# Joining the small matmul bursts of a fused attention and Winograd-MoE kernel: values and next scores side by side at eleven of fifteen places

## The chip, the cores and the metric

The kernel runs on one core of a Trainium2 chip. The metric is the device time of one execution in microseconds (us). The kernel before took 674.62 us (median of three runs, 672.25 to 675.16). A smaller number is better.

## The reference

Eight batches of eight heads of attention over 576 positions, head size 64, with one of two sparse causal masks: heads 0 to 3 look back at most 31 positions (local), heads 4 to 7 look at positions with the same remainder by 32 (strided). The result goes through a layer with three input matrices, an elementwise maximum and one output matrix.

```python
def _attn_ref(q, k, v):
    B, H, S, D = q.shape                      # 8, 8, 576, 64
    stride, scale = 32, 1.0 / np.sqrt(D)
    scores = scale * np.matmul(q, k.transpose(0, 1, 3, 2))
    ...
    mask_local = (rel >= 0) & (rel < stride)
    mask_strided = (rel >= 0) & (pos[None, :] % stride == pos[:, None] % stride)
    ...
    scores = np.where(masks[None, :, :, :], scores, -1000000000.0)
    scores = scores - np.max(scores, axis=-1, keepdims=True)
    attn = np.exp(scores)
    attn = attn / (np.sum(attn, axis=-1, keepdims=True) + 1e-09)
    return np.matmul(attn, v).astype(np.float32)

def _moe_ref(x, w1, w2, w3, w_out):           # x: 4608 x 512, d_ff 768
    h = np.maximum(np.maximum(x @ w1, x @ w2), x @ w3)
    return (h @ w_out).astype(np.float32)
```

## The kernel before

**Units.** The attention is cut into 32 units, unit n being batch n // 4 and one pair of heads; units with n % 4 of 0 and 1 are strided, with 2 and 3 local. A unit goes through these steps, each a function of the kernel:

- `scores(n)`: a burst of 64 small matmuls (strided, line 314, tiles of 64 rows x 64 columns of the array) or 72 (local, line 336, 64 x 32) into the one PSUM tile `s_ps`;
- `less_maximum(n)` on DVE: add the mask (L357), take the maximum (L365), subtract it (L366);
- `exponentials(n)` on ACT (L382);
- `probabilities(n)` and `transposed(n)` on DVE: sum (L393), two small steps (L394, L395), multiply (L396), transpose into `pt` (L403), after which `s_ps` is free for the next unit;
- `values(n)`: a burst of 64 small matmuls (strided, L469, tiles 64 x 64) or 84 (local, L440, 32 x 64) into `o_ps`;
- `leading(n)` on ACT: copies of `o_ps` to the block of the layer's input (L494).

Ahead of a strided unit's scores, `paired_queries` makes four copies on ACT (L291).

**Supers.** Tokens 1024 to 4607 go through the layer in four supers of 896 tokens. A super has nine quads, and a quad is seven products (a Winograd form of a 2 x 2 block product), so a super has 63 products, numbered k = 0 to 62. One product is six matmuls of 128 x 128 weights against 448 columns (line 788). Products alternate between two PSUM banks, and ACT copies each result out (`snap`, L835, or L842): a product two places on writes the same bank and waits for that copy. The fourth, fifth and sixth products of a quad (k % 7 of 3, 4, 5) also have an addition on POOL (L847) behind the copy; in quads with q % 3 of 1 or 2 DVE takes a running maximum (L849) after that addition, and after the copy of the seventh. After quad 7 (after product 55) `split` casts two pieces of the hidden layer on ACT (L872) and DVE (L873). After the 63 products come the 126 output matmuls of a super (L882), with the conversion of the next super's input beside them.

**Order.** Every instruction is pinned to the order in which the program is written, on each engine. What places the late units (16 to 31) among the products is `before(s, k)`, called ahead of product k of super s, and `after(s, k)`, called behind it and ahead of that product's copy. With `COUNTS = (6, 6, 4, 0)`, `before` puts the scores of unit n + 1 ahead of product 8, 17, 26, 35, 44 and 53 (`k % 9 == 8`, lines 799 to 803) and the values of unit n one product later (lines 804 and 805). `after` puts the exponentials two products behind the scores, the probabilities and the transpose three behind, and the paired queries four behind (lines 811 to 817). Loads of queries, keys and values go out on SP's queue beside these steps, between the loads of the products' weights (`load_next`), which run eight ahead.

Of the kernel before, what the change touches and what calls it, by code (L numbers as in the profile page):

```python
# [37 lines left out]
NBLOCK = (B * S - PLAIN) // BL  # L38
NSUPER = NBLOCK // 2
AHEAD = 8  # L40
COUNTS = (6, 6, 4, 0)
W_LEAST = 2.0**-15
W_MOST = 122877.984375
NKC = DM // P
# [26 lines left out]
def fused_kernel(ctx, tc, qT, kT, qk_loc, qk_str, v_loc, v_str, m_loc, m_str, w1, w2, w3, w_out, out):  # L71
# [158 lines left out]
    units = [(b, p) for b in range(B) for p in (2, 3, 0, 1)]  # L230
# [420 lines left out]
    def ahead(n):  # L651

        scores(n)
        list(load_qk(n + 2))
        less_maximum(n)
# [66 lines left out]
    coming, since = None, 0  # L722
# [59 lines left out]
    def supers():  # L782
# [9 lines left out]

        def before(s, k):

            n = 16 + sum(COUNTS[:s]) + (k - 8) // 9
            if s == 0 and k == 1:
                ahead(16)
                running[:] = [16, k]
            elif k % 9 == 8 and k // 9 < COUNTS[s]:
                running[:] = []  # L800
                if n + 1 < len(units):
                    ahead(n + 1)
                    running[:] = [n + 1, k]
            elif k and k % 9 == 0 and k // 9 <= COUNTS[s]:
                placed(n)

        def after(s, k):

            if running:
                n, since = running  # L810
                if k == since + 2:
                    exponentials(n)
                if k == since + 3:
                    probabilities(n)
                    transposed(n)
                if k == since + 4 and n + 1 < len(units) and (n + 1) % 4 in (0, 1):
                    paired_queries(n + 1)

        def quad(s, q):
            _, j, i = builds[q]  # L820
# [69 lines left out]
            pin(nc.scalar.dma_start(out=out[r : r + P, :], in_=o_sb))  # L890

        running = []
        for s in range(NSUPER):
            for q in range(9):
                quad(s, q)
                if q == 7:
                    split(0, 0, 4)
                    split(1, 0, 4)
            split(2, 0, 4)
            split(0, 4, 6)  # L900
            split(1, 4, 6)
            split(2, 4, 6)
            convert = conversion(s + 1) if s + 1 < NSUPER else iter(())
            out_part(0, 0, 4)
            out_part(1, 0, 4)
            for t in range(7):
                out_part(t, 0 if t > 1 else 4, 6)
                store(s, t)
                if t < 4:
                    split(t + 3, 0, 6)  # L910
                next(convert, None)
            list(convert)
# [68 lines left out]
```

## Time and profile before

| | |
|---|---|
| median of three runs | 674.62 us (672.25 to 675.16) |
| the profiled execution | 670.4 us, of which the span of instructions is 668.6 us |
| PE (matmul) busy | 644.8 us, 96% of the span |
| PE weight loads busy | 552.2 us, 83% |
| DVE, ACT, POOL busy | 372.6, 336.6, 300.0 us: 56%, 50%, 45% |
| line 788, the products | 1512 matmuls, 317.4 us |
| granted TensorE clock, mean | 0.989 |

The profiled execution is 4.2 us below the median of the three runs. The page's busy time of PE counts matmuls from their start to a modelled end, and these overlap, so the distances from start to start in a timeline say more than busy shares. PE, DVE, ACT, POOL and SP are the engines; PEld is PE's weight load, which runs beside matmuls. A super's products stand at 203 to 296 us, 325 to 417, 446 to 531 and 560 to 636 of the span; the late units stand in the first three.

### The profile page before, as it was taken

How to read it: one execution, taken by the hardware profiler on the slowest of the kernel's cores; microseconds unless marked ns; L12 is line 12 of the kernel's file. 1: busy time of each engine (PE TensorE's matmuls, PEld its weight loads, DVE VectorE, ACT ScalarE, POOL GpSimd, SP SyncE). 2: the span in 40 equal slices, each digit the busy share in tenths (PEclk: the TensorE clock that was granted, in tenths of full speed). 3: DMA queues.
4: the chain of work that ended last, by engine and by line, in shares of the span. 5: the costliest groups of instructions: out<-in, count | busy, mean ns of one | idle time of the engine just before them, and what ended most of it. 6: DMA issues, size and time to landing. Idle time of an engine off the chain costs nothing.

```text
span 668.6 us, 18029 instructions
## 1 busy us (share of the span) xinstructions
PE 644.8 (96%) x7408; PEld 552.2 (83%) x7408; DVE 372.6 (56%) x515; ACT 336.6 (50%) x702; POOL 300.0 (45%) x291
## 2 busy tenths in 40 slices
PE   4589999999999999999999999999999999999997
PEld 3467888878778888888888888888899888999986
DVE  5887877576675566476255756643652562214240
ACT  5767566335264455456445455544454554444441
POOL 7879999699942334230224233004324401444410
PEclk9789999999999999999999999999999999999999
DMA  9989885657699778761477898228767614777411
GB/s 291 271 231 367 269 257 177 210 165 234 188 296 334 248 245 276 238 228 63 132 240 256 227 296 250 75 96 223 229 175 212 204 63 125 216 217 216 125 47 64
DMA packets 89370, 138.36 MB, mean 207 GB/s; under 512 B 10152, under 2 KB 39592, under 8 KB 89288
## 3 DMA queue, kind: packets, MB, share of 16 engines
q1 hardware_dynamic: 85256, 129.86, 63.0%
q10 hardware_dynamic: 4032, 7.34, 2.9%
q8 instruction: 59, 0.97, 0.6%
q14 instruction: 23, 0.19, 0.1%
HBM read 111.21 MB, written 25.95 MB: 205 GB/s over the span
## 4 chain that ended last, share of the span: by engine, by line
PE 93%; ACT 2%; DVE 1%; issue 1%; DMA 1%; POOL 1%; SPq 1%; DVEq 0%; ACTq 0%; POOLq 0%
PE f_ps L788 46%; PE f_ps L882 17%; PE f_ps L521 15%; PE f_ps L551 4%; PE o_ps L440 3%; PE o_ps L469 2%; PE s_ps L314 2%; PE s_ps L336 2%; DMA w<-in_w 1%; ACT s_ps L374 1%; DVE o_ps L179 0%; DVE work L182 0%; DMA v_t<-in_v_loc 0%; PE o_ps L480 0%; SPq L265 0%
## 5 line engine op out<-in xcount | busy, mean ns | idle before, releaser
L788 PE MATMUL f_ps<-xc,w_stream 128*128 128x448 f32 x1512 | 317.4, 368 | 0.2 <-ACT snap L835 0.2
L788 PEld LDWEIGHTS f_ps<-xc,w_stream 128*128 128x128 f32 x1512 | 280.5, 188 | 26.3 <-ACT snap L835 1.8
L835 ACT COPY snap<-f_ps 128x448 f32<-128x448 f32 x240 | 128.0, 534 | 164.6 <-PE f_ps L788 162.4
L847 POOL TENSOR_TENSOR snap<-snap 128x448 f32<-128x448 f32 x72 | 88.9, 1240 | 148.8 <-ACT snap L835 122.5
L849 DVE TENSOR_TENSOR h_all<-h_all,snap 128x448 f32<-128x448 f32 x96 | 81.1, 886 | 128.9 <-POOL snap L847 128.9
L847 POOL TENSOR_TENSOR h_all<-snap 128x448 f32<-128x448 f32 x36 | 41.4, 1150 | 167.5 <-ACT snap L835 166.3
L882 PE MATMUL f_ps<-wNone,h_parts 128*128 128x512 f32 x504 | 115.0, 389 | 0.0
L882 PEld LDWEIGHTS f_ps<-wNone,h_parts 128*128 128x128 f32 x504 | 94.6, 188 | 19.6
L521 PE MATMUL f_ps<-xh,w 128*128 128x512 f32 x288 | 95.1, 401 | 0.4 <-issue 0.4
L521 PEld LDWEIGHTS f_ps<-xh,w 128*128 128x128 f32 x288 | 54.7, 190 | 13.0 <-issue 0.6
L521 PE MATMUL f_ps<-xl,w 128*128 128x512 f32 x144 | 56.8, 394 | 0.4 <-DVE xl L499 0.4
L873 DVE TENSOR_TENSOR h_parts<-h_all,h_parts 128x768 fp32r<-128x768 f32 (+2 forms) x40 | 27.2, 712 | 30.3 <-ACT h_parts L872 30.2
L888 ACT COPY work<-f_ps 128x512 f32<-128x512 f32 x28 | 16.4, 587 | 46.1 <-PE f_ps L882 46.1
L685 DVE TENSOR_TENSOR xc<-x_block,xc 128x896 fp32r<-128x896 f32 x28 | 29.8, 1087 | 11.7 <-ACT xc L682 11.7
L393 DVE TENSOR_REDUCE s_ps<-s_ps 128x10 f32<-128x640 f32 (+2 forms) x30 | 23.1, 772 | 19.4 <-ACT s_ps L382 19.4
L403 DVE STREAM_TRANSPOSE pt<-s_ps 128x640 f32<-128x640 f32 (+2 forms) x32 | 32.5, 1016 | 1.2
L521 PEld LDWEIGHTS f_ps<-xl,w 128*128 128x128 f32 x144 | 27.3, 190 | 5.9 <-DVE xl L499 0.7
L382 ACT ACTIVATE s_ps<-s_ps 128x640 f32<-128x640 f32 (+2 forms) x30 | 19.5, 649 | 22.2 <-DVE s_ps L366 22.2
L872 ACT CAST h_parts<-h_all 128x768 fp32r<-128x768 f32 (+2 forms) x40 | 24.5, 643 | 12.1 <-DVE h_all L849 5.5
L551 PE MATMUL f_ps<-wNone,hh 128*128 128x512 f32 x96 | 30.6, 400 | 0.0
L682 ACT CAST xc<-x_block 128x896 fp32r<-128x896 f32 x28 | 25.7, 943 | 5.4 <-DVE x_block L688 3.0
L336 PEld LDWEIGHTS s_ps<-qk_t 64*32 64x32 f32 x1408 | 16.2, 114 | 14.2 <-issue 13.5
(87 smaller groups left out, 680.2 us busy)
## 6 DMA issues: line engine op xcount, KB each, us to landing
w_stream<-scratch SPq DMA_DIRECT2D x252, 256.0 KB, 3.5
w<-in_w SPq DMA_DIRECT2D x18, 512.0 KB, 7.5
qk_t<-in_qT SPq DMA_DIRECT2D x28, 288.0 KB, 3.5
qk_t<-in_kT SPq DMA_DIRECT2D x28, 288.0 KB, 5.3
v_t<-in_v_str SPq DMA_DIRECT2D x56, 128.0 KB, 4.5
out<-work ACTq DMA_DIRECT2D x28, 256.0 KB, 2.0
scratch<-w SPq DMA_DIRECT2D x27, 256.0 KB, 3.8
v_t<-in_v_loc SPq DMA_DIRECT2D x48, 96.0 KB, 3.9
```

What stands on the lines that cost most here:

```text
L336: pin(nc.tensor.matmul(s_ps[32 * j : 32 * (j + 1), h, k1 : k1 + w], t[hs, q0 : q0 + 32], t[hs, k0 : k0 + w], start=not first, stop=not fir ...
L403: pin(nc.vector.transpose(pt[:, :, : nm * at], s_ps[:, :, : nm * at]))
L521: pin(nc.tensor.matmul(f_ps, w[:, kc, :], x[:, kc, :], start=(kc == 2 and n == 0), stop=(kc == 1 and n == 2)))
L551: pin(nc.tensor.matmul(f_ps, h[:, ts], w, start=(j == 0 and n == 0), stop=(j == NJ - 1 and n == 2)))
L682: pin(nc.scalar.copy(out=x[m][:, 0], in_=src))
L685: pin(nc.vector.tensor_tensor(out=x[m][:, 1], in0=src, in1=x[m][:, 0].bitcast(F32), op=ALU.subtract))
L788: pin(nc.tensor.matmul(out_, w[:, wl, fs], x[:, xl, k, :], start=start and k == 0 and n == 0, stop=k == 1 and n == 2, skip_group_check=not ...
L835: pin(nc.scalar.copy(out=t, in_=src))
L847: pin(nc.gpsimd.tensor_tensor(out=h if i == 0 else u, in0=u, in1=t, op=ALU.add))
L849: pin(nc.vector.tensor_tensor(out=h, in0=h, in1=u, op=ALU.max))
L873: pin(nc.vector.tensor_tensor(out=to[:, 1, j0:j1], in0=src, in1=to[:, 0, j0:j1].bitcast(F32), op=ALU.subtract))
L882: pin(nc.tensor.matmul(outs[t], h, w, start=(j == 0 and n == 0), stop=(j == NJ - 1 and n == 2)))
```

## The change

`COUNTS` goes; two tables of numbers, `SCORES_AT` and `VALUES_AT`, say per super ahead of which product a unit's scores and a unit's values stand, the units numbered from 16 in the order of the tables. Where the same product stands in both tables (11, 24, 44, 54 in super 0; 11, 27, 47, 57 in super 1; 10, 18, 29 in super 2), `before` now issues the values of unit n and then the scores of unit n + 1 with nothing between them; behind both come the loads of values, the copies of `leading`, the loads of queries and keys, and `less_maximum`. At the four other places (units 18 and 19, 21 and 22, 23 and 24, 25 and 26) the scores still come first and one product stands between. Within a super the scores of a unit stand 7 to 13 products behind those of the unit before. The scores of unit 22 and values of unit 21 move from the end of super 0 to the start of super 1. The arithmetic is unchanged. Line numbers after the change are up to nine higher (788 is 789, 314 is 315, 469 is 470).

```diff
--- before.py
+++ after.py
@@ -38,7 +38,8 @@
 NBLOCK = (B * S - PLAIN) // BL
 NSUPER = NBLOCK // 2
 AHEAD = 8
-COUNTS = (6, 6, 4, 0)
+SCORES_AT = ((1, 11, 24, 33, 44, 54), (0, 11, 18, 27, 36, 47, 57), (10, 18, 29))
+VALUES_AT = ((11, 24, 34, 44, 54), (1, 11, 19, 27, 37, 47, 57), (10, 18, 29, 37))
 W_LEAST = 2.0**-15
 W_MOST = 122877.984375
 NKC = DM // P
@@ -792,17 +793,19 @@
 
         def before(s, k):
 
-            n = 16 + sum(COUNTS[:s]) + (k - 8) // 9
-            if s == 0 and k == 1:
-                ahead(16)
-                running[:] = [16, k]
-            elif k % 9 == 8 and k // 9 < COUNTS[s]:
-                running[:] = []
-                if n + 1 < len(units):
-                    ahead(n + 1)
-                    running[:] = [n + 1, k]
-            elif k and k % 9 == 0 and k // 9 <= COUNTS[s]:
-                placed(n)
+            n, new = values_at.get((s, k)), scores_at.get((s, k))
+            if n is not None:
+                values(n)
+            if new is not None:
+                scores(new)
+                running[:] = [new, k]
+            if n is not None:
+                list(load_v(n + 2))
+                leading(n)
+                rest(n)
+            if new is not None:
+                list(load_qk(new + 2))
+                less_maximum(new)
 
         def after(s, k):
 
@@ -815,6 +818,8 @@
                     transposed(n)
                 if k == since + 4 and n + 1 < len(units) and (n + 1) % 4 in (0, 1):
                     paired_queries(n + 1)
+                if k == since + 4:
+                    running.clear()
 
         def quad(s, q):
             _, j, i = builds[q]
@@ -890,6 +895,10 @@
             pin(nc.scalar.dma_start(out=out[r : r + P, :], in_=o_sb))
 
         running = []
+        scores_at, values_at = (
+            {at: 16 + i for i, at in enumerate((s, k) for s, ks in enumerate(places_) for k in ks)}
+            for places_ in (SCORES_AT, VALUES_AT)
+        )
         for s in range(NSUPER):
             for q in range(9):
                 quad(s, q)
```

Three places where the order of instructions moves:

On PE in super 0, the first place with two bursts before (ahead of products 8 and 9): L788 is a product, L314 the scores of unit 17, L469 the values of unit 16.

```order
L788 MATMUL f_ps_781<-xc_2966,w_stream 128x448 x6
L314 MATMUL s_ps<-qk_t,pt 64x2x18 x32
L788 MATMUL f_ps_782<-xc_2967,w_stream 128x448 x6
L469 MATMUL o_ps<-pt,v_t 64x2x18 x32
L788 MATMUL f_ps_781<-xc_2968,w_stream 128x448 x6
L788 MATMUL f_ps_782<-xc_2969,w_stream 128x448 x6
L788 MATMUL f_ps_781<-xc_2970,w_stream 128x448 x6
```

The same two bursts after the change, ahead of product 11 (product 8 is the first row):

```order
L789 MATMUL f_ps_782<-xc_2967,w_stream 128x448 x6
L789 MATMUL f_ps_781<-xc_2968,w_stream 128x448 x6
L789 MATMUL f_ps_782<-xc_2969,w_stream 128x448 x6
L470 MATMUL o_ps<-pt,v_t 64x2x18 x32
L315 MATMUL s_ps<-qk_t,pt 64x2x18 x32
L789 MATMUL f_ps_781<-xc_2970,w_stream 128x448 x6
L789 MATMUL f_ps_782<-xc_2971,w_stream 128x448 x6
```

The product that stood between the bursts now stands outside, the values come first, and both bursts are of tiles 64 x 64.

On ACT around product 55 of super 0, before: L494 the copies of unit 21, L382 the exponentials of unit 22, L872 the two casts behind quad 7, L835 the copies of products.

```order
L494 COPY x_block_3347<-o_ps 128x384
L494 COPY x_block_4130<-o_ps 128x192
L835 COPY snap<-f_ps_782 128x448
L382 ACTIVATE s_ps<-s_ps 128x2x320
L835 COPY snap<-f_ps_781 128x448
L872 CAST h_parts<-h_all 128x512 x2
L835 COPY snap<-f_ps_782 128x448
```

After the change, where unit 21 has its scores ahead of product 54 (L495 the copies of unit 20, L383 the exponentials of unit 21, L877 the casts):

```order
L495 COPY x_block_3330<-o_ps 128x384
L495 COPY x_block_4187<-o_ps 128x192
L840 COPY snap<-f_ps_782 128x448
L840 COPY snap<-f_ps_781 128x448
L877 CAST h_parts<-h_all 128x512 x2
L383 ACTIVATE s_ps<-s_ps 128x32x18
L840 COPY snap<-f_ps_782 128x448
L840 COPY snap<-f_ps_781 128x448
```

The casts and the exponentials had a copy of a product between them; now they stand back to back, with the copy of product 56 behind both.

On DVE in super 1, unit 23 before (L357 to L366 its maximum, L849 the running maximum of the hidden layer, L393 to L403 its probabilities and transpose), with its scores ahead of product 8:

```order
L357 TENSOR_TENSOR s_ps<-s_ps,mloc 128x2x320
L365 TENSOR_REDUCE mx<-s_ps 128x2x5
L366 TENSOR_TENSOR s_ps<-s_ps,mx 128x2x320
L849 TENSOR_TENSOR h_all<-h_all,snap 128x448
L393 TENSOR_REDUCE s_ps<-s_ps 128x2x5
L394 TENSOR_SCALAR s_ps<-s_ps 128x2x5
L395 RECIPROCAL sm<-s_ps 128x2x5
L396 TENSOR_TENSOR s_ps<-s_ps,sm 128x2x320
L403 STREAM_TRANSPOSE pt<-s_ps 128x2x320
L849 TENSOR_TENSOR h_all<-h_all,snap 128x448 x3
```

After the change, with its scores ahead of product 11:

```order
L854 TENSOR_TENSOR h_all<-h_all,snap 128x448
L358 TENSOR_TENSOR s_ps<-s_ps,mloc 128x2x320
L366 TENSOR_REDUCE mx<-s_ps 128x2x5
L367 TENSOR_TENSOR s_ps<-s_ps,mx 128x2x320
L854 TENSOR_TENSOR h_all<-h_all,snap 128x448 x3
L394 TENSOR_REDUCE s_ps<-s_ps 128x2x5
L395 TENSOR_SCALAR s_ps<-s_ps 128x2x5
L396 RECIPROCAL sm<-s_ps 128x2x5
L397 TENSOR_TENSOR s_ps<-s_ps,sm 128x2x320
L404 STREAM_TRANSPOSE pt<-s_ps 128x2x320
L854 TENSOR_TENSOR h_all<-h_all,snap 128x448
```

One running maximum (of product 10) now stands ahead of the unit's own maximum, and three (of products 11, 12, 13) instead of one ahead of its probabilities.

## Rows read from the trace of the kernel before

**Rows 1.** The page: busy time of each engine (share of the span, instructions), and the share of the chain of waits that ended last, by engine.

```profile
PE 644.8 (96%) x7408; PEld 552.2 (83%) x7408; DVE 372.6 (56%) x515; ACT 336.6 (50%) x702; POOL 300.0 (45%) x291
...
PE 93%; ACT 2%; DVE 1%; issue 1%; DMA 1%; POOL 1%; SPq 1%; DVEq 0%; ACTq 0%; POOLq 0%
```

**Rows 2.** The waits of PE's matmuls, and then of its weight loads, from 204 to 640 us: engine, line, waited for; us in total, times, the longest.

```profile
PE f_ps L788 <- ACT snap L835: 0.2, 1, 0.2
```

```profile
PEld o_ps L469 <- issue: 2.5, 8, 0.3
...
PEld f_ps L788 <- ACT snap L835: 1.8, 6, 0.5
```

**Rows 3.** The timeline of PE around two places in super 0 (start, length with the modelled end, instructions merged): the scores of units 21 and 22, the values of units 20 and 21.

```profile
268.39 1.14 PE L314 MATMUL s_ps<-qk_t,pt 64*64 64x36 f32 x64
269.46 1.50 PE L788 MATMUL f_ps<-xc,w_stream 128*128 128x448 f32 x6
270.89 1.14 PE L469 MATMUL o_ps<-pt,v_t 64*64 64x36 f32 x64
271.95 9.99 PE L788 MATMUL f_ps<-xc,w_stream 128*128 128x448 f32 x48
281.88 0.97 PE L336 MATMUL s_ps<-qk_t 64*32 64x64 f32 x72
282.78 1.49 PE L788 MATMUL f_ps<-xc,w_stream 128*128 128x448 f32 x6
284.19 1.14 PE L469 MATMUL o_ps<-pt,v_t 64*64 64x36 f32 x64
```

**Rows 4.** The same view of super 3, whose 63 products have no burst among them.

```profile
559.64 76.78 PE L788 MATMUL f_ps<-xc,w_stream 128*128 128x448 f32 x378
636.26 1.09 PE L882 MATMUL f_ps<-wNone,h_parts 128*128 128x512 f32 x4
```

**Rows 5.** The same view at 58 us, in an earlier stage of the kernel, where two small bursts of the same tile stand side by side (L521 is that stage's large matmul).

```profile
58.25 1.14 PE L314 MATMUL s_ps<-qk_t,pt 64*64 64x36 f32 x64
59.20 1.12 PE L469 MATMUL o_ps<-pt,v_t 64*64 64x36 f32 x64
60.25 0.50 PE L521 MATMUL f_ps<-xh,w 128*128 128x512 f32 x1
```

**Rows 6.** The timeline of ACT from product 54 of super 1 (idle time and its releaser in brackets): exponentials of unit 28, casts behind quad 7, paired queries.

```profile
407.37 0.53 ACT L835 COPY snap<-f_ps 128x448 f32<-128x448 f32 x1 [0.52 <-PE f_ps L788]
407.80 0.65 ACT L382 ACTIVATE s_ps<-s_ps 128x576 f32<-128x576 f32 x1
408.64 0.53 ACT L835 COPY snap<-f_ps 128x448 f32<-128x448 f32 x1 [0.20 <-PE f_ps L788]
409.07 1.15 ACT L872 CAST h_parts<-h_all 128x512 fp32r<-128x512 f32 x2
410.12 0.53 ACT L835 COPY snap<-f_ps 128x448 f32<-128x448 f32 x1
410.54 1.34 ACT L291 COPY pt<-qk_t 128x288 f32<-128x288 f32 x4
411.77 1.01 ACT L835 COPY snap<-f_ps 128x448 f32<-128x448 f32 x2
```

**Rows 7.** The waits of the weight loads in the stretch of rows 6 (402 to 414 us) and in the one around unit 23 (334 to 350 us).

```profile
PEld f_ps L788 <- ACT snap L835: 0.5, 1, 0.5
```

```profile
PEld f_ps L788 <- ACT snap L835: 0.3, 1, 0.3
```

**Rows 8.** Unit 23 in super 1 before: PE's scores; then ACT, the copy of the product ahead of them, the exponentials, and the copies on both sides of the paired queries; then DVE, a running maximum, the first step of the probabilities and the transpose.

```profile
334.85 0.97 PE L336 MATMUL s_ps<-qk_t 64*32 64x64 f32 x72
```

```profile
334.96 0.53 ACT L835 COPY snap<-f_ps 128x448 f32<-128x448 f32 x1 [0.68 <-PE f_ps L788]
...
340.23 0.70 ACT L382 ACTIVATE s_ps<-s_ps 128x640 f32<-128x640 f32 x1
...
342.23 0.53 ACT L835 COPY snap<-f_ps 128x448 f32<-128x448 f32 x1 [0.73 <-PE f_ps L788]
...
343.90 0.53 ACT L835 COPY snap<-f_ps 128x448 f32<-128x448 f32 x1
```

```profile
342.82 0.63 DVE L849 TENSOR_TENSOR h_all<-h_all,snap 128x448 f32<-128x448 f32 x1 [4.40 <-POOL snap L847]
343.37 0.82 DVE L393 TENSOR_REDUCE s_ps<-s_ps 128x10 f32<-128x640 f32 x1
...
345.56 0.85 DVE L403 STREAM_TRANSPOSE pt<-s_ps 128x640 f32<-128x640 f32 x1
```

**Rows 9.** Durations from 204 to 500 us: POOL's addition (count, busy us, mean ns, idle before and releaser).

```profile
L847 POOL TENSOR_TENSOR snap<-snap 128x448 f32<-128x448 f32 x45 | 55.1, 1228 | 104.0 <-ACT snap L835 93.3 <-issue 10.0
```

**Rows 10.** DVE at unit 22 in super 0 before, where a running maximum stands ahead of the unit's own, and at unit 21, a strided one, from its sum to its transpose.

```profile
283.82 0.62 DVE L849 TENSOR_TENSOR h_all<-h_all,snap 128x448 f32<-128x448 f32 x1 [5.83 <-POOL snap L847]
284.37 0.83 DVE L357 TENSOR_TENSOR s_ps<-s_ps,mloc 128x640 f32<-128x640 f32 x1
...
286.09 0.83 DVE L366 TENSOR_TENSOR s_ps<-s_ps,mx 128x640 f32<-128x640 f32 x1
```

```profile
274.64 0.77 DVE L393 TENSOR_REDUCE s_ps<-s_ps 128x16 f32<-128x576 f32 x1 [2.69 <-ACT s_ps L382]
...
276.75 1.25 DVE L403 STREAM_TRANSPOSE pt<-s_ps 128x1024 f32<-128x1024 f32 x1
```

## The prediction

> **What bounds the kernel now.** I read the page first: PE is busy for 96% of the span and 93% of the chain that ended last is PE's own work [rows 1], so time is won only where PE's instructions stand closer together. Then the waits: from 204 to 640 us PE's matmuls wait 0.2 us in all, and its weight loads about 0.3 us at each small burst, for nothing that the profile shows ("issue"), and 1.8 us in six waits for ACT's copies [rows 2]. So the loss at a burst is no wait for data; it has to be read from distances in PE's timeline. Super 3 has 63 products and no burst: 636.26 - 559.64 = 76.62 us, 1.216 us a product [rows 4]. A product between two bursts takes 270.89 - 269.46 = 1.43 and 284.19 - 282.78 = 1.41 us, and eight products between two places 281.88 - 271.95 = 9.93 us, where 8 x 1.216 is 9.73 [rows 3]. Each stretch of products that a burst cuts off thus costs 0.20 us, whatever its length. That is the price that the change can save: a place with both bursts together leaves one stretch fewer.
>
> **The joined places.** Eleven places lose the lone product between their bursts; it moves into a long stretch, where it costs 1.216 us. That alone is 1.42 - 1.216 = 0.20 us a place. What comes on top depends on the seam between the two bursts. Rows 5 show one: 64 score matmuls and 64 value matmuls, both in 64 x 64 tiles, side by side take 0.95 + 1.05 = 2.00 us, where two bursts apart take 1.07 + 1.06 = 2.13 [rows 3, 5]. So a seam of one tile saves a further 0.13: 0.33 a place. Four places are of that kind (units 16/17, 20/21, 24/25, 28/29: strided values, then strided scores): 1.32 us.
>
> The other seven change the tile at the seam: 64 x 64 to 64 x 32 (17/18, 29/30), 32 x 64 to 64 x 64 (19/20, 27/28), 32 x 64 to 64 x 32 (22/23, 26/27, 30/31). No row shows such a seam without another wait in it. Bounds: as smooth as rows 5, 0.33 saved; or the seam costs as much as a whole cut between burst and product, 0.20, and nothing is saved. I take 0.20, that the first burst keeps its tail of 1.07 us and the lone product's excess goes: 7 x 0.20 = 1.40 us. [...] Sum of the joined places: 2.72 us saved, from 1.3 to 3.6.
>
> **What moves on ACT.** ACT copies a product out and the product two places on waits for that copy. Copies come every 1.216 us. One that starts 0.26 us late (410.12 - 408.64 = 1.48) brought no wait; 0.45 late (343.90 - 342.23 = 1.67) brought 0.3 us; 0.70 late (411.77 - 408.64 = 3.13 against 2.43) brought 0.5 us [rows 6, 7, 8]. The paired queries cause most of these; they are still four products behind the scores, and I leave those waits as they are. One gets better: unit 28 had its paired queries right behind the two casts of quad 7 in super 1 [rows 6]; at product 57 they are clear of the casts, 0.5 becomes 0.3, 0.2 us saved. One new wait comes: unit 21 at product 54 of super 0 has its exponentials two products on, behind the two casts. From the start of the copy of product 55, a copy's slot of 0.43 (409.07 - 408.64), the casts 1.05 (410.12 - 409.07) and the exponentials 0.65 [rows 6] put the next copy at 2.13 instead of 1.22, 0.91 late. By the two waits above, that is about 0.6 to 0.7 us; I take 0.6 lost, from 0.3 (the shorter wait) to 0.8.
>
> **What moves on DVE.** Counted from the end of a joined burst, products end at 1.32 (1.216 and 0.10, half a cut), 2.54 and 3.75, and a copy starts 0.2 behind a product's end (0.11 behind a burst's start, which is itself half a cut late, 334.96 against 334.85) [rows 3, 8]. The exponentials, now behind the second product alone, can start at about 3.2; before, the values' burst and one cut more stood in that stretch, 1.07 and 0.2 us. A unit's own maximum takes 286.09 + 0.83 - 284.37 = 2.55 us on DVE [rows 10]. At units 18, 20, 25, 27, 28, 29 and 31 no running maximum is left ahead of it, and it ends at 2.6. At 17, 21, 23 and 30 one of the last product stands ahead, behind a copy and an addition of 1.23 us [rows 9]: 0.2 + 0.53 + 1.23 + 0.62 = 2.6 us after that product [rows 6, 9, 10], and as the joined burst covers 2.0 of them, the unit's maximum ends at about 0.6 + 2.55 = 3.2. Both are in time, so exponentials cost nothing; the cover is the joined burst itself.
>
> Two distances get short. Scores of unit 24 stand seven products behind those of 23 and need `s_ps`, free after the transpose. Exponentials from 3.2 to 3.9, then the copy of product 13, and three running maxima ahead of the probabilities, the second behind an addition (3.2 to 4.45) and the third behind that: about 5.8. From the sum to the transpose's end is 345.56 + 0.85 - 343.37 = 3.04 us [rows 8], so 8.8 to 9.0. The burst is due after seven products: 1.32 + 6 x 1.216 = 8.62, with the paired queries' wait and half a cut 8.9: a wait of 0 to 0.3. The values of unit 29 stand eight products behind its scores, ahead of product 18 of super 2: the addition of product 12 from 4.4 to 5.6, its maximum to 6.3, and 276.75 + 1.25 - 274.64 = 3.36 [rows 10] makes 9.7, due at 9.9: 0 to 0.2. I take 0.2 us lost for both.
>
> Loads on SP's queue keep the weights eight ahead, as before; they wait for the same bursts, and no wait of PE names them [rows 2]. I cost them at nothing; a late one would cost what PE then waits.
>
> **The sum.** -2.72 - 0.2 + 0.6 + 0.2 = -2.1 us. The profiled execution of 670.4 us becomes 668.3. It was 4.2 us faster than the median of the three runs, 674.62, so in their terms the time is 672.5 us, 0.31% less.
>
> **Rivals.**
> - *All seams are smooth.* If the small tiles follow each other like rows 5 whatever their shape, the places save 11 x 0.33 = 3.6 us, and if exponentials and transposes are in time everywhere but for 0.3 at unit 21, the sum is -3.6 - 0.2 + 0.3 = -3.5: 671.1 us. For it: nothing in rows 5 shows a seam at all. Against it: the cut of 0.20 us at every change of tile in rows 3.
> - *The change does not do what it says.* The second burst waits inside a joined place, or a changed tile costs a whole cut: seven places save nothing, and the two short distances and unit 21 cost their upper ends. -1.3 - 0.2 + 0.8 + 0.5 = -0.2: 674.4 us. For it: the 4.4 and 9.9 us above leave little room. Against: values now stand eight or more products behind their scores nearly everywhere.
> - *The unit's maximum is late, and ACT stands.* DVE works in order, and the exponentials are asked for 1.27 us sooner. At unit 22 a running maximum put the unit's own to 284.37, 1.5 us behind its burst of 0.9 us (281.88 to 282.78 and its tail), so that it ended 4.1 us behind [rows 3, 10]. Were that so at all eleven places, exponentials would run from 4.1 to 4.8 and the copy that should start at 3.95 would be 0.8 late: some 0.6 us each, 6.6 in all, and with the sum above +4.5: 679.1 us, slower. It decides from a maximum that ends 3.55 us behind the burst, where the copy is 0.3 late. Against it: only four places have a running maximum ahead, and the joined burst is 1.1 us longer than that single one.
>
> **How the numbers follow.** The forecast of 672.5 us has a chance of 0.52, the smooth seams 0.20, the spoilt gain 0.21, the late maximum 0.07. About 0.5%, 3.4 us, is what a measurement of this kernel tells from no change. The forecast and the spoilt gain lie within it; the smooth seams lie just past it. So faster 0.23, same 0.70, slower 0.07. The forecast's own range goes from 3.6 + 0.2 - 0.3 = 3.5 us saved to 0.2 saved, 671.1 to 674.4; the three runs of before spread from 2.4 below their median to 0.5 above, so I add 1.3 below and 0.8 above: 669.8 to 675.2 us. The late maximum is left out.
>
> **What would show it.** Right: in super 0 the value matmuls of unit 16 start 0.95 us ahead of unit 17's scores, and 2.0 us are between the first and the product behind; at a changed tile the first burst takes about 1.07 us (0.9 to 1.0 if smooth, 1.2 or more if a whole cut). A stretch of ten to twelve products is still 0.20 us above 1.216 each. A wait of a weight load for a copy of about 0.6 us stands at product 58 of super 0, and a weight load of scores or values waits for DVE's transpose ahead of product 18 in supers 1 and 2. Wrong: more waits for ACT's copies than the seven or so that there were, with exponentials that wait for L367, or a changed gap in a super that has no burst.

## The result, and the profile after

| | before | after |
|---|---|---|
| median | 672.25 us (11 runs, 669.95 to 675.96) | 676.97 us (11 runs, 673.5 to 682.37) |
| ratio to before | | 1.0067, 95% interval 1.0044 to 1.009 |
| profiled execution, its span | 670.4, 668.6 us | 677.43, 675.7 us |
| first product of super 0 to the end of the span | 465.93 us | 469.13 us |
| mean granted clock | 0.989 | 0.982 |

The kernel became 0.67% slower; 672.5 us, 0.31% less than before, was forecast, and 676.97 lies above the range. A second profile of each (runs e8 and e4 below) gives 466.68 us for the part from the first product on before, 470.24 after. So the late part lost 3.2 to 3.6 us. What stands ahead of the first product has the same code in both kernels and took 202.71 and 205.40 us before, 206.56 and 204.13 after; in the six other kernels below that leave it as it is, it took 202.9 to 206.8. That difference is between executions, and it is left out from here on. "The rest" below is the part from the first product on. From 203 to 642 us the granted clock is 1.00 in both kernels, so the clock is no part of the loss.

The page of after: busy times and chain, to set beside [rows 1], and two lines of its table of DMA queues (packets, MB, share). The kernel before has the same packets and MB for q8:

```profile
PE 646.8 (96%) x7408; PEld 555.8 (82%) x7408; DVE 370.8 (55%) x515; ACT 336.5 (50%) x702; POOL 300.5 (44%) x291
...
q1 hardware_dynamic: 85256, 129.86, 61.4%
...
q8 instruction: 59, 0.97, 0.6%
...
PE 91%; DMA 3%; DVE 2%; issue 2%; SPq 1%; ACT 1%; POOL 1%; ACTq 0%; POOLq 0%
```

PE's share of the chain fell from 93 to 91%, and "issue" rose from 1 to 2%. Where that is, the waits of PE's matmuls and of its weight loads tell, from 208 to 642 us (columns as in [rows 2]):

```profile
PE s_ps L337 <- issue: 2.0, 1, 2.0
PE f_ps L789 <- issue: 1.8, 2, 1.3
PE o_ps L470 <- DVE pt L404: 0.5, 1, 0.5
PE o_ps L441 <- issue: 0.3, 1, 0.3
PE f_ps L789 <- ACT snap L840: 0.2, 1, 0.2
```

```profile
PEld f_ps L789 <- ACT snap L840: 1.9, 6, 0.6
PEld o_ps L470 <- DVE pt L404: 0.9, 1, 0.9
PEld s_ps L315 <- DVE pt L404: 0.5, 1, 0.5
```

Before, PE's matmuls had one wait of 0.2 us in this stretch [rows 2]. Now four waits for "issue", nothing that the profile shows, hold 4.1 us, and one for DVE's transpose 0.5. The weight loads' waits for ACT's copies are six of 1.9 us in all, where they were six of 1.8 before. The timeline of PE shows three of the four stops, all at joined places, or in the product behind one (columns as in [rows 3], idle time and releaser in brackets):

```profile
268.73 1.14 PE L441 MATMUL o_ps<-pt,v_t 32*64 32x64 f32 x84
269.81 1.14 PE L315 MATMUL s_ps<-qk_t,pt 64*64 64x36 f32 x64
270.88 1.28 PE L789 MATMUL f_ps<-xc,w_stream 128*128 128x448 f32 x5
272.58 11.56 PE L789 MATMUL f_ps<-xc,w_stream 128*128 128x448 f32 x55 [0.43 <-issue]
...
396.45 1.14 PE L441 MATMUL o_ps<-pt,v_t 32*64 32x64 f32 x84
397.52 0.95 PE L337 MATMUL s_ps<-qk_t 64*32 64x64 f32 x71
400.50 0.24 PE L337 MATMUL s_ps<-qk_t 64*32 64x64 f32 x1 [2.02 <-issue]
...
476.31 1.14 PE L470 MATMUL o_ps<-pt,v_t 64*64 64x36 f32 x64 [0.48 <-DVE pt L404]
477.38 0.97 PE L337 MATMUL s_ps<-qk_t 64*32 64x64 f32 x72
478.28 1.69 PE L789 MATMUL f_ps<-xc,w_stream 128*128 128x448 f32 x7
481.29 2.90 PE L789 MATMUL f_ps<-xc,w_stream 128*128 128x448 f32 x13 [1.32 <-issue]
```

At 398 us PE has issued 71 of 72 score matmuls, and the last one comes 2.0 us later, for nothing that the profile shows. The fourth stop (0.27 us) is within the values of unit 23 at 356 us, where no two bursts stand side by side. Measured from the start of one instruction to the start of the next, the four are 0.79, 0.48, 2.24 and 1.69 us; less the usual distances (0.04 in a burst, 0.20 in a product) they come to 4.7 us. The rest without them is 469.13 - 4.7 = 464.4 us, 1.5 less than before.

**What the four have in common.** I put PE's instructions, weight loads, matmuls and the few semaphore instructions, in order of their start and counted them from 0: 15,113. All four stops come behind the instruction whose number leaves 192 when divided by 256. And 15,113 / 256 is 59.0, the number of packets of queue q8, "instruction"; 0.97 MB / 59 is 16.4 KB a packet. The 59 packets come while the program runs: in the records of q8 the first starts at 9.59 us and the last at 659.46 us of the span. The records of one packet can be bracketed by the view of DMA queues, here from 396.4 to 398.1 us and then from 398.1 to 399.1 us:

```profile
q1 hardware_dynamic: 223, 0.39, 69.7%
```

```profile
q1 hardware_dynamic: 10, 0.02, 6.2%
q8 instruction: 1, 0.02, 5.8%
```

In the first of these the loads take 69.7% of the DMA engines' time, and no instruction packet comes; in the second, in which PE already stands, one packet comes and little else; PE goes on at 400.50 us. My theory A from here: PE's instructions come in pieces of 256, and where PE uses up a piece before the packet that it then needs has come, it stands. A strided burst is 128 instructions, 64 matmuls and their 64 weight loads, a local one 144 or 168, so a joined place holds 256 to 312, and PE goes through them in 2 us; a product of 1.2 us has 12. So a piece that falls into a joined place is short. Rival B: something in a joined place itself, the seam, its loads or its place, stops PE.

### The profile page after: what moved, and what is told of

It reads as the page before. It is cut to its first block, busy times and chain, and to the rows that moved or that the text cites. A ratio compares the mean times of both kernels' runs of the same rounds, so it can differ in the third digit from the quotient of the medians.

```text
span 675.7 us, 18036 instructions
## 1 busy us (share of the span) xinstructions
PE 646.8 (96%) x7408; PEld 555.8 (82%) x7408; DVE 370.8 (55%) x515; ACT 336.5 (50%) x702; POOL 300.5 (44%) x291
## 3 DMA queue, kind: packets, MB, share of 16 engines
q1 hardware_dynamic: 85256, 129.86, 61.4%
## 4 chain that ended last, share of the span: by engine, by line
PE 91%; DMA 3%; DVE 2%; issue 2%; SPq 1%; ACT 1%; POOL 1%; ACTq 0%; POOLq 0%
PE f_ps L789 44%; PE f_ps L887 17%; PE f_ps L522 16%; PE f_ps L552 5%; PE o_ps L441 3%; DMA w<-in_w 2%; PE o_ps L470 2%; PE s_ps L315 2%; PE s_ps L337 2%; DMA v_t<-in_v_str 1%; DVE h_all L854 1%; SPq L243 1%; POOL snap L852 1%; PE o_ps L481 0%; SPq L152 0%
## 5 line engine op out<-in xcount | busy, mean ns | idle before, releaser
L854 DVE TENSOR_TENSOR h_all<-h_all,snap 128x448 f32<-128x448 f32 x96 | 79.5, 868 | 140.7 <-POOL snap L852 140.7
L522 PE MATMUL f_ps<-xh,w 128*128 128x512 f32 x288 | 96.8, 407 | 0.0
L893 ACT COPY work<-f_ps 128x512 f32<-128x512 f32 x28 | 16.4, 586 | 44.0 <-PE f_ps L887 44.0
L877 ACT CAST h_parts<-h_all 128x768 fp32r<-128x768 f32 (+2 forms) x40 | 24.5, 642 | 14.3 <-DVE h_all L854 7.7
L383 ACT ACTIVATE s_ps<-s_ps 128x640 f32<-128x640 f32 (+2 forms) x30 | 19.5, 649 | 22.2 <-DVE s_ps L367 22.2
L337 PEld LDWEIGHTS s_ps<-qk_t 64*32 64x32 f32 x1408 | 16.4, 114 | 16.9 <-issue 16.3
L337 PE MATMUL s_ps<-qk_t 64*32 64x64 f32 (+1 forms) x1408 | 19.5, 228 | 11.0 <-DMA qk_t<-in_kT 8.2
```

Of the source, the lines that this page charges most:

```text
L337: pin(nc.tensor.matmul(s_ps[32 * j : 32 * (j + 1), h, k1 : k1 + w], t[hs, q0 : q0 + 32], t[hs, k0 : k0 + w], start=not first, stop=not fir ...
L522: pin(nc.tensor.matmul(f_ps, w[:, kc, :], x[:, kc, :], start=(kc == 2 and n == 0), stop=(kc == 1 and n == 2)))
L854: pin(nc.vector.tensor_tensor(out=h, in0=h, in1=u, op=ALU.max))
L877: pin(nc.scalar.copy(out=to[:, 0, j0:j1], in_=src))
```

## Experiments

Each run's "rest" and its stops (PE's distance from start to start at the end of a piece, less the usual one, summed over the products) are worked out from its trace as above.

### The kernels again (e4, e8)

> The changed kernel once more, unchanged. Theory A: the stops stand at the same four places as in its first profile, since the stream is the same: 469 us from the first product to the end, within 1.5. The time ahead of the first product (206.6 us then, 202.7 before the change), where the two kernels are equal, is run to run and may be anywhere from 202 to 210. Theory C (chance meetings of loads): other places, other sums.

> The kernel before once more, for a second profile: from the first product to the end 465.9 us within 0.7, no stop over 0.4 us at the end of a piece in the supers (theory A), and the time ahead of the first product anywhere from 202 to 207 us: if it is as high here as in the changed kernel's profiles (204.1 and 206.6), that stretch is no part of the change.

e4: 676.08 us, rest 470.24, stops at 269.5, 353.8, 381.1, 396.4 and 477.4 us (distances of 0.78, 0.43, 0.48, 1.89 and 2.25 us; 5.3 in all, less the usual ones): the same four pieces and one more. e8: 673.82 us, rest 466.68, no stop. The places belong to the program, their lengths vary.

### The same order of bursts, the pieces shifted (e1, e2)

```diff
-S0 A0 S1 X0 ...
+S0 A0 P40 S1 X0 ...
+    def turns(n):
+        for _ in range(n):
+            pin(nc.tensor.matmul(o[:32, 0, :18], unit[:32, :32], unit[:32, :18], start=True, stop=True))
```

`P40` puts 40 tiny matmuls into the opening (160 instructions of PE); e2 has `P30` (120).

> The changed kernel with 40 tiny matmuls (32 rows, 18 columns, results unused; 80 weight loads and 80 matmuls as the trace counts them, so 160 instructions of PE) in the opening, where PE waits for the first queries. Everything behind them is the same, but stands 160 instructions later in PE's stream. Theory A (PE's instructions come in pieces of 256; a joined burst uses up a piece in 2 to 3 us, faster than the next one comes, and PE stops at the piece's end): the four long stops of the profile (0.6, 0.4, 2.0 to 2.2, 1.5 us, all at instruction numbers 192 modulo 256) vanish, because the pieces' ends now fall into stretches of products; no piece is used up in under 3.75 us. From the first product to the end of the span about 464.5 us instead of 469.1 (before: 465.9), and about 4.5 us faster than the changed kernel, 0.2% faster than before. Theory B (the stops belong to the joined bursts themselves or to the loads beside them, at whatever place in the stream): the stops stay at the same bursts, 469 us from the first product on, ratio to before 1.007.

> The same with 30 tiny matmuls, 120 instructions of PE. Theory A: the pieces' ends fall into other joined bursts than in the changed kernel; the old four stops vanish and six others come, near unit 17 to 18 in super 0 (2.1 us), product 57 of super 0 (0.9), units 22 to 23 (1.75) and 27 to 28 (1.75) in super 1, units 28 to 29 (1.1) and 30 to 31 (2.2) in super 2: 9.8 us in all. From the first product to the end about 474 us, ratio to before about 1.013 to 1.018, and some 10 us above the kernel with 160. Theory B: as that kernel, 469 us.

e1: 679.73 us, ratio 1.0121 (1.0094 to 1.0149), rest 467.32, stops 2.7 us. e2: 680.78 us, ratio 1.0157 (1.0114 to 1.02), rest 469.36, stops 4.7 us. Both are slower through the opening (first product at 211.52 and 215.41 us), where there are stops too. In the supers of e1 three of the four old places have no stop. At the fourth, product 47 of super 1, PE now stands 160 instructions sooner, within the values of unit 26 instead of at the end of unit 27's scores, and three more stops stand elsewhere, again all at 192 of 256. Two of them in PE's timeline of e1, within the values of unit 26 and the scores of unit 28:

```profile
400.69 1.03 PE L441 MATMUL o_ps<-pt,v_t 32*64 32x64 f32 x75
402.63 0.32 PE L441 MATMUL o_ps<-pt,v_t 32*64 32x32 f32 x9 [0.91 <-issue]
402.88 0.97 PE L337 MATMUL s_ps<-qk_t 64*32 64x64 f32 x72
...
417.47 0.65 PE L315 MATMUL s_ps<-qk_t,pt 64*64 64x36 f32 x26
418.93 0.78 PE L315 MATMUL s_ps<-qk_t,pt 64*64 64x36 f32 x38 [0.81 <-issue]
```

No burst was moved in the supers, so B cannot move the stops; A says that they go with the count. A's sizes were wrong in both: e1 has four stops for which I had none, since I took it that a long piece is always in time, and the gain that I had is not there; e2 has about half of what I had, and of the six places that I named three have a stop, while three others have one that I did not name. So the count says where a stop can be, and not whether it comes.

### The bursts apart again at three places, at all, and joined at the old places (e3, e5, e6)

```diff
 e3, values of units 19, 26 and 29:
-VALUES_AT = ((11, 24, 34, 44, 54), (1, 11, 19, 27, 37, 47, 57), (10, 18, 29, 37))
+VALUES_AT = ((11, 24, 34, 45, 54), (1, 11, 19, 27, 37, 48, 57), (10, 19, 29, 37))
 e5:
+VALUES_AT = ((12, 25, 34, 45, 55), (1, 12, 19, 28, 37, 48, 58), (11, 19, 30, 37))
 e6:
+SCORES_AT = ((1, 8, 17, 26, 35, 44, 53), (8, 17, 26, 35, 44, 53), (8, 17, 26))
+VALUES_AT = ((8, 17, 26, 35, 44, 53), (8, 17, 26, 35, 44, 53), (8, 17, 26, 35))
```

> The changed kernel with three of the eleven joined places taken apart, those at which the profile shows the long stops: ahead of product 44 of super 0, 47 of super 1 and 18 of super 2 the scores stand first, and the values one product later, as in the kernel before. Theory A: the piece ends there take 1.4 us longer to reach, so the stops at 44 and 18 go and the one at 47 shrinks from 2.0 to 0.8 us; three lone products cost 0.2 us each and the one smooth seam does not exist there: about 469.1 - 3.3 + 0.7 = 466.5 us from the first product on. Theory B (a joined place costs what it costs, and here three of eleven are undone; the loss of 3.2 us is spread over all): about 468 us.

> The changed kernel's places, but no two bursts joined: the scores stand where they stood in the change and the values one product later at all places. Theory A (the loss is PE waiting at the end of a piece of 256 instructions, because a joined burst uses a piece up in 2 to 3 us): no such stop over 0.4 us, save one at most; the eleven lone products cost 0.2 us each again; the wait of the values of unit 29 for its transpose goes; the waits at unit 21 and 24 stay (0.5 and 0.2). From the first product to the end 466 to 467 us, against 465.9 before and 469 to 470 for the change: the loss is gone, ratio to before 1.000 to 1.003. Theory B (the new places are what costs: exponentials behind casts, short distances on DVE, loads at other times): 469 us or more, ratio 1.007 or more.

> The places of the kernel before (every nine products from 8), all fifteen joined: the values and the next scores ahead of the same product. Theory A: fifteen seams save 0.2 to 0.33 each, some 3.5 us, and fifteen joined bursts meet the ends of pieces: 5 to 7 us of stops; a few waits for transposes, as nine products are less far than before: 467 to 471 us from the first product on, slower than before by 0.3 to 0.8%. Theory B: the joining saves 3.5 us: 463 us, ratio 0.994.

e3: 677.98 us, ratio 1.0089 (1.0062 to 1.0115), rest 471.59, stops 5.3 us: one at each of the three places that were pulled apart (0.46, 1.09 and 2.50 us), and one of 1.59 at product 24 of super 0, which is still joined. e5: 674.82 us, ratio 1.0023 (1.0002 to 1.0043), rest 467.93, three stops, 1.8 us, with no joined place at all; A had one at most. Its scores stand where after has them and its values at most one product later, so the new places alone are not the bulk of the loss. e6: 675.36 us, ratio 1.0034 (1.0005 to 1.0063), rest 473.53, seven stops, 8.0 us; its profiled execution, 680.36 us, was the slowest of ten, so this rest is high for the kernel. One product between the bursts does not cure a stop: in e3 the piece at the place in super 2 still lasts only 3.28 us. So what counts is not the seam. e3 speaks against B, since places that are apart again still have stops, and was a miss for me as well, who had placed a cure there.

### Fewer instructions at the joined places (e7)

```diff
+        wide_few = n >= 17 and n not in (19, 22, 24, 26)
+        for m in range(2 if wide_few else 0):
+            pin(nc.tensor.matmul(s_ps[:, m, :256], t[:, :P], t[:, S : S + 256], start=True, stop=True))
-        for m in range(MS if pairs else 0):
+        for m in range(MS if pairs and not wide_few else 0):
```

> The changed kernel with the scores of the eleven joined places computed by two wide matmuls (128 rows, 256 columns of queries against keys, eight instructions of PE with the weight loads) instead of 64 or 72 small ones: the scores of these units are not the reference's, everything else and all loads stay. PE has some 1400 instructions fewer and about the same work: the two wide ones take about 1 us as well (0.6 to 1.7). Theory A: a joined place no longer uses up a piece, the stops go: from the first product on 464.5 us and eleven times what the wide pair takes more or less than 1 us. Theory B (loads or the joined places themselves): PE waits for nothing shown at the same bursts, 469 us.

669.31 us, ratio 0.9939 (0.9913 to 0.9965), rest 463.04, no stop at all. A joined place of e7 in PE's timeline, and its line of instruction packets:

```profile
392.69 1.14 PE L444 MATMUL o_ps<-pt,v_t 32*64 32x64 f32 x84
393.76 1.13 PE L311 MATMUL s_ps<-qk_t 128*128 128x256 f32 x4
394.54 5.62 PE L792 MATMUL f_ps<-xc,w_stream 128*128 128x448 f32 x26
```

```profile
q8 instruction: 53, 0.87, 0.6%
```

The wide matmuls take nearly as long (0.78 us, 394.54 - 393.76 here, and up to 0.09 more in the product behind, against 0.90 for 72 small ones and 1.05 to 1.07 for 64); over the eleven places PE has some 0.9 us less work (both bursts and the product behind take 35.8 us, 36.8 in after without its stops there). Places, loads and DVE's steps are those of after. With 1400 instructions fewer (six packets) the stops are gone and the rest is 6.1 us shorter than after's: 4.7 of stops, 0.9 of work, and 0.5 that I cannot place. It computes something else, so it is no better kernel, but it separates the count from the place.

### The old order with the pieces shifted (e11)

`P37`, 148 instructions, in the kernel before; the diff is that of e1.

> The kernel before, no burst moved, with 37 tiny matmuls (148 instructions of PE) ahead of the first scores of the opening, so that the ends of pieces of 256 instructions fall 148 instructions earlier in the supers. Theory A: six pieces come to 2.9 to 3.5 us (at the values of units 19, 21, 22, 27, 28 and 30), and three to six of them have a stop at their end, 0.2 to 1.5 us each, 2 to 6 us in all, in a kernel with no joined place. Theory B: nothing in the supers is changed, so no stop there, as in both profiles of the kernel before; the time differs by the tiny matmuls (some 2 us) and the opening alone.

679.82 us, first product at 211.60, rest 466.51, one stop: 0.34 us within the values of unit 18, at the end of a piece of 8.9 us whose packet started 6.8 us in. It is at none of the six places named, which have no stop, so A as it stood failed here. Six pieces did come to 2.87 to 3.31 us, as worked out, but their packets had come early. So a short piece is not enough; the packet's time must be looked at too.

**The packets.** That is what a table over all 13 profiles does, worked out from the records of queue q8 and of PE. From the first product to the last lie 419 pieces. At the ends of 43 of them PE stands more than 0.3 us, and in every one it goes on 1.21 to 1.60 us (median 1.40) after the end of the packet. At the other 376 the packet had ended 1.45 us or more before PE came to the end of the piece, but for nine (1.02 to 1.41 us ahead, PE's distance there 0 to 0.25 us). Some of them, times from the end of the piece before:

```
kernel  near us   piece used by   packet starts  ends   PE goes on
after    271.8        2.86            1.42       2.30      3.65
after    356.2        6.20            4.33       5.28      6.68
after    398.3        1.60            1.47       2.40      3.84
after    479.6        3.08            2.32       3.41      4.77
before   271.8        3.32           -0.41       0.53      3.33
before   245.8        4.29            1.59       3.13      4.53
before   473.7        4.36            1.35       2.63      4.36
before   257.3       11.55            7.98       8.98     11.55
```

("near" is where the piece ends; in a product PE goes on 0.20 behind the end of a piece anyway, as 0.24 at 245.8 us.) Before has short pieces as well, but none under 3.3 us among the products, and where one was short its packet was early enough; at 245.8 us it was near the edge. After has pieces of 1.6 to 3.1 us. Over all profiles 37 pieces last under 3.5 us, and 19 of them end in a stop; the other 24 stops end longer pieces, with packets that started 2.1 to 12 us in.

### The loads later (e10)

```diff
-                list(load_v(n + 2))
+                owed.append((2, load_v, n + 2))
...
-                list(load_qk(new + 2))
+                owed.append((4, load_qk, new + 2))
```

`after` issues what is owed that many products later.

> The kernel after with the loads of values issued two products later and those of queries and keys four later. If the loads behind the joined places hold up the instruction packets and by that cause the stops: the packets behind the joined places start within 3 us of the piece's end (8 to 10 us in the kernel after), and the four stops (0.79, 0.48, 2.24, 1.69) are gone or below 0.4 us each; rest 464 to 465. If the stops come from the short pieces alone (1.6 to 3.1 us for 256 instructions, against some 3.7 that a piece needs from the end of one to the next): the stops at products 44, 47 and 18 of supers 0, 1, 2 stay at 0.5 to 2.3 us, whatever the later packets do; at most the one of 0.48 at unit 23's values goes; rest 468 to 469.5.

687.91 us (one run), rest 482.41, seven stops, 12.0 us, up to 3.46. Neither of the two came about: the packets behind the joined places start later still (12.05, 13.56 and 13.88 us behind the piece's end, where after has 8.71, 10.37 and 9.91), and the stops at the three products grew to 1.6, 3.3 and 3.5 us. Packets seem to come when the loads issued just before are done, for they moved by 3.2 to 4.0 us with loads that moved by 2.4 to 4.9; that is argued from one run. If so, the loads have a part in when a packet comes; to issue them later is no cure. A kernel without those loads was not tried.

### Places chosen by pieces (e9)

```diff
+SCORES_AT = ((0, 10, 20, 29, 39, 49, 59), (0, 10, 20, 32, 42, 57), (5, 15, 28))
+VALUES_AT = ((10, 20, 31, 39, 49, 59), (2, 10, 20, 30, 42, 57), (5, 15, 28, 42))
```

> Other tables, nothing else: twelve of the fifteen places joined, units 9 to 15 products apart, each place chosen so that no 256 instructions of PE in a row (counted from the same start as in the kernel after) take under 4.0 us, worked out from 1.216 us a product, 0.20 a cut and the measured bursts; scores and values at least 10 products apart, no scores ahead of products 52 to 56. Theory A (the stops come from instructions fetched 256 at a time): no stop over 0.3 us, or one, in the supers; the part from the first product to the end is 465.9 to 466.7 in the kernel before and 464.4 to 464.9 in the one after without its stops; less one more place (0.2 to 0.3) and the waits at unit 21, values of 29 and scores of 24 (about 1.0), it is 463 to 464, and the ratio to the kernel before 0.994 to 0.997. Theory B (joined bursts themselves, or the loads issued behind them, stop PE): more joined places than in the kernel after, so 4 to 6 us of stops again and a ratio of 1.004 to 1.010.

671.59 us (12 runs; before 672.51 beside it), ratio 0.9994 (0.9971 to 1.0016), rest 464.31. Twelve places are joined, one more than in after, and the "issue" waits of PE's matmuls from 203 to 640 us are down from 4.1 to 0.7 us:

```profile
PE f_ps L887 <- ACT h_parts L877: 0.5, 1, 0.5
PE s_ps L337 <- issue: 0.4, 1, 0.4
PE s_ps L315 <- issue: 0.3, 1, 0.3
```

The place of unit 26's values, where after stood longest, in e9's timeline:

```profile
388.18 1.14 PE L441 MATMUL o_ps<-pt,v_t 32*64 32x64 f32 x84
389.25 0.97 PE L337 MATMUL s_ps<-qk_t 64*32 64x64 f32 x72
390.15 18.68 PE L789 MATMUL f_ps<-xc,w_stream 128*128 128x448 f32 x90
```

B had 4 to 6 us of stops and a ratio of 1.004 or more here; it falls. A had none or one stop over 0.3 us and 463 to 464 us; there are two (0.58 and 0.54, the packets 6.7 and 8.6 us late), and the rest is 0.3 longer. Against after this order wins back the loss; against before the gain of 1.6 us in the rest of one profile is within what the runs can tell, and the forecast ratio was missed. No order tried is shown to beat the kernel before.

## Why the prediction was wrong, point by point

- **What bounds the kernel.** Right as far as it went: PE's instructions had to stand closer, and the price of a cut holds. Ten products between two places of after take 396.45 - 384.09 = 12.36 us, 0.20 above ten times 1.216:

```profile
384.09 12.43 PE L789 MATMUL f_ps<-xc,w_stream 128*128 128x448 f32 x60
```

- **The step that failed** is the sum, "-2.72 - 0.2 + 0.6 + 0.2 = -2.1 us". It takes it that "time is won only where PE's instructions stand closer together" and has no term for PE running out of instructions when they do; without a reason that stood at nothing. It was 4.7 us in the profile of after and 5.3 in the second, against 2.1 forecast to be won, as both bursts side by side use up a piece in 1.6 to 3.1 us. The trace of before had the sign of it: q8's 59 packets on the page, 15,114 instructions, and "issue" as the releaser. It even had the stops, ahead of the window of [rows 2], in the opening, where PE stands 0.8 to 3.2 us at four ends of pieces and goes on 1.31 to 1.51 us after the end of the packet. The longest cuts a burst of 128 matmuls in two:

```profile
27.32 0.78 PE L480 MATMUL o_ps<-pt,v_t 18*64 18x18 f32 x59 [1.50 <-ACT s_ps L374]
31.09 1.26 PE L480 MATMUL o_ps<-pt,v_t 18*64 18x18 f32 x69 [3.00 <-issue]
```

- **The joined places.** Right. With one tile, unit 16's values start 222.45 - 221.49 = 0.96 us ahead of unit 17's scores, and 2.01 us are between the first and the product behind:

```profile
221.49 1.14 PE L470 MATMUL o_ps<-pt,v_t 64*64 64x36 f32 x64
222.45 1.12 PE L315 MATMUL s_ps<-qk_t,pt 64*64 64x36 f32 x64
223.50 12.83 PE L789 MATMUL f_ps<-xc,w_stream 128*128 128x448 f32 x62
```

  A changed tile keeps the first burst's tail: 269.81 - 268.73 = 1.08 and 397.52 - 396.45 = 1.07 us in the fences above; all seven changed tiles have 1.07 to 1.08, the four seams of one tile 0.95 to 0.96. So the seven save 0.20 each, which was my choice between two bounds, and not 0.33, and the smooth seams fall as a rival.
- **ACT.** Right. The wait at product 58 of super 0 is there, 0.6 us of a weight load; in start-to-start distances it cost 0.42 and 0.10 more in the next product, 0.6 forecast. Unit 28's wait of 0.5 [rows 7] became 0.2, 0.3 forecast. Casts, exponentials and the late copy:

```profile
289.33 1.14 ACT L877 CAST h_parts<-h_all 128x512 fp32r<-128x512 f32 x2
290.37 0.64 ACT L383 ACTIVATE s_ps<-s_ps 128x576 f32<-128x576 f32 x1
290.94 0.97 ACT L840 COPY snap<-f_ps 128x448 f32<-128x448 f32 x2
```

- **DVE.** The waits stand where they were forecast. Scores of unit 24 lost 0.25 us (0 to 0.3). Values of unit 29 lost 0.55 (0 to 0.2), which was mis-sized: two running maxima ahead of the probabilities took 2.09 us together, one of them 1.56, where [rows 8] show 0.63, and the transpose ended at 475.00 + 1.25 = 476.25, about 10.4 us behind the burst that ends at 465.83, where 9.7 was forecast.

```profile
470.89 2.09 DVE L854 TENSOR_TENSOR h_all<-h_all,snap 128x448 f32<-128x448 f32 x2 [1.05 <-POOL snap L852]
472.90 0.75 DVE L394 TENSOR_REDUCE s_ps<-s_ps 128x16 f32<-128x576 f32 x1
...
475.00 1.25 DVE L404 STREAM_TRANSPOSE pt<-s_ps 128x1024 f32<-128x1024 f32 x1
```

- **The loads at nothing.** No wait of PE names one, as said. Queue q1, with the loads in it, has 61.4% of the DMA engines' time on the page and the instruction packets 0.6%, and four packets of after that follow such loads started 8 to 10 us behind the end of a piece. But those pieces lasted 13 to 16 us, and no stop came of it; at after's four stops the packet started 1.4, 4.3, 1.5 and 2.3 us behind the end of the piece before. That the loads have a part in these starts is not shown; all that is shown is e10's one run, in which later loads came with longer stops.
- **The sum without its stops.** -2.72 - 0.3 + 0.5 + 0.55 + 0.25 is -1.7 us, and the rest without its stops is 1.5 us (464.4 against 465.93) and 1.8 us (464.9 against 466.68) shorter; with the two profiles of each paired the other way, 1.0 and 2.3. So the terms that it had held to about half a microsecond, and one missing term of 4.7 to 5.3 turned it: -1.5 + 4.7 = 3.2 us.
- **The rivals.** The late maximum, my only one on the slower side, did not come: six waits for ACT's copies, no more than before. The spoilt gain had a second burst that waits inside a joined place, and the longest stop, 2.24 us in the scores of unit 27, is one; but that rival named no cause for such a wait and let it cost no more than the saving. That the kernel is slower has a cause that none of the rivals named.

## What to carry to other kernels

In these runs PE's instructions were traffic as well, 59 packets of 16.4 KB in after. Where a page has packets on the instruction queue, count the engine's instructions (weight loads too), and before placing two bursts of small matmuls side by side work out how long each piece of them, 256 here, would last. Here PE needed the packet to have ended some 1.4 us before a piece was used up, so pieces under 3.5 us stood at risk (19 of 37 ended in a stop), and longer ones too where the packet came late. The four waits for "issue" came back at the same places in e4, and three of them were gone in e1, with the pieces shifted by 160 instructions. Where a wait comes back like that, number the instructions and look for a common remainder, and choose places by it, as in e9 (0.7 us of such waits against 4.1), or spend fewer instructions on the burst, as in e7 (no stop). Look for such waits in the whole span of the kernel before, and not only in the stretch that is changed.

## What the runs showed of the hardware

- A packet of 16.4 KB took 0.88 to 2.2 us (median 0.99). Of the 419 above, 201 started 0.5 to 2.5 us behind the end of the piece before, 62 ahead of it, and 48 started 8 to 14 us behind it. 41 of these 48 stand among the units' bursts and loads, the other seven (8.1 to 9.0 us) behind the last unit. What sets that start, and why it came early in e11, stays open.
- In e10 PE stood 3.46 us ahead of 488.5 us, and the granted clock of the stretch behind is 0.50 (columns: stretch, its length, busy time of PE, PEld, DVE, ACT and POOL, granted clock, DMA share, GB/s):

```profile
480.00:485.00 5.00, 4.52 (x150) 3.85 (x149) 3.93 (x5) 1.77 (x4) 1.23 (x1) 1.00 0.99 289
485.00:488.50 3.50, 0.57 (x3) 0.18 (x1) 2.29 (x4) 0.53 (x1) 1.13 (x1) 0.94 0.65 203
488.50:493.00 4.50, 4.24 (x11) 3.79 (x12) 0.00 (x0) 1.13 (x2) 0.95 (x1) 0.50 0.37 90
```

  The next two whole products behind the stop take 2.38 and 2.24 us instead of 1.216. In e6, too, the granted clock is 0.57 from 234 to 238 us, behind a stop of 2.73, and in e3 0.50 from 482.5 to 485.5 us, behind one of 2.50. It did not go by the length of the stop alone in these runs: behind 1.58 us in e6 and 1.82 in e10 the clock fell to 0.50 as well (412 to 415 and 386 to 389 us), while behind the stop of 2.24 in after it stayed at 1.00 (400.5 to 404 us), and behind the one of 1.69 too (482 to 486 us). So this is no part of after's loss; of the losses of e3, e6 and e10 it is.
